# The first chunk of a fused recurrence and its inverse put ahead of the weight conversion in the opening

## The chip, the cores and the metric

The kernel runs on one core of a Trainium2 chip. The metric is the device time of one execution in microseconds (us). The core has a matrix engine (TensorE, PE), a vector engine (VectorE, DVE), a scalar engine (ScalarE, ACT), GpSimd (POOL) and SyncE (SP). They run their own instruction streams in order and wait for each other by semaphores. SP issues most transfers; ScalarE has a queue of its own for transfers too.

## The reference

Three parts follow each other. First a recurrence over 768 time steps for 4 batches and 8 heads with a 40 by 40 state, then two feed-forward parts on the 3072 tokens that it gives.

```
for t in range(S):                       # S = 768
    y[:, :, t] = r_t . state
    Sa = state . a_t
    state = state * w_t - outer(Sa, b_t) + outer(v_t, k_t)
x = y as 3072 x 320
x = ((x @ w_a) * (x @ w_b)) @ w_out      # w_a, w_b: 320 x 1536
out = gate * relu(x @ w1[e]) @ w2[e]     # e: the best of 8 experts of each token
```

## The kernel before, in words

The recurrence is computed in 12 chunks of 64 steps. What chunk c needs ahead of the state, the class `Attention` makes: it loads `w` and makes running products of it (`scans`, lines 493 to 498, DVE); scales `a` on POOL (`scale_a`) and spreads it by three transfers for each pair of batches into `ablk`; scales `bk` (`scale_bk`, line 527, DVE); multiplies them on PE (`scores`, line 537), copies the result out on ScalarE (line 545), masks it on POOL, and sends it to HBM (`nd`, line 552). From there it comes back in another layout as `m` (lines 600 and 605). `tinv` then inverts a triangular matrix by 31 pairs of a product and a difference on DVE (lines 614 and 620, so 62 steps that wait for each other); its result leaves through HBM (`td`, line 631) and comes back into `s` (line 635). `t21a` and `t21b` (a transpose on DVE at line 651, and products on PE) complete the inverse. `rows` makes transposed copies (`kb`), `relayout` moves running products into `gp` by six transfers, and `spans` checks on ScalarE that `w` lies in a range (line 474).

With these, `stage0` to `stage5` carry the state through chunk c for each of the four batches, mostly on PE, and give the tokens of the chunk (`xf`, line 816). The up-projection of a finished chunk, in groups of eight products (line 966), runs on PE while the next chunk goes through the recurrence; ScalarE copies one half out (line 969) and DVE multiplies it with the other (`uh`, line 978).

The weights `w_a` and `w_b` have to be split once into a high and a low part. `split64` does that in 30 pieces of 128 by 256, each in four steps on DVE (lines 364, 367, 376, 378), with a square, a check and casts on ScalarE (lines 365, 372, 374) and two instructions on POOL (380, 386). These are the 120 steps called `conv`. Raw data of a piece is loaded on ScalarE's queue into one of two or three buffers, so one or two pieces ahead.

`phase1` writes the order of the instructions by hand: first an opening, then a loop over the chunks, with 24 slots each. What stands in which slot is set by the tables STEADY and, for chunk 0, FIRST: `conv` says how many conversion steps, `tinv` how many steps of an inverse a slot holds; the conversion ends when its 120 steps are used up. In the opening before, 75 conversion steps are run, in part dealt between the steps of the inverses of chunks 0 and 1, which are both finished there; the other 45 follow in the loop, nearly all within chunk 0. Instructions of PE, DVE, ScalarE and POOL stay in this order; transfers on SP are put in order by a scheduler, and each of them uses one of eight completion lanes in turn and waits until the transfer before it on that lane has landed.

Of the kernel before, what the change touches and what calls it, by code (L numbers as in the profile page):

```python
# [21 lines left out]
C = 64  # L22
# [110 lines left out]
def phase1(tc, I, cst, drm, psA, psM, ident, hT, mk_ident, wo, xs, span, tiny, down):  # L133
# [66 lines left out]
    units, tinv = [], []  # L200
    for c in range(NCH + 1):
# [9 lines left out]
        for i in range(24):  # L211
# [76 lines left out]
            if 2 <= c < 10 and i == T["fill"]:  # L288
                if c == 2:
# [4 lines left out]
                    zt[:, None, :].to_broadcast([128, 2 * nz // XW, XW // 2]))  # L294
            n = T["tinv"][i]
# [14 lines left out]
    if not down:  # L310
# [40 lines left out]
def split64(nc, pool, raw, his, lo, dups=(), small=None):  # L351
# [1375 lines left out]
```

## Time and profile before

| | us |
|---|---|
| median of three runs | 1339.77 |
| lowest and highest | 1337.69, 1344.06 |
| the profiled execution | 1347.63 |
| its span, first to last instruction | 1345.9 |
| PE busy in the span | 1195.2 (89%) |
| DVE busy | 695.7 (52%) |
| ACT busy | 533.6 (40%) |
| POOL busy | 443.6 (33%) |

The profile is of one execution. Busy time is the time in which an engine ran an instruction; waiting and issuing of transfers are not counted. The median of the runs is the number to compare with; all shorter times are read from the profiled execution.

### The profile page before, as it was taken

The page shows a single profiled execution, that of the slowest core. Times are in us where ns is not written, and L with a number is a line of the kernel's source. Part 1 is how long each engine was busy: PE and PEld are TensorE (multiplying, and loading weights), DVE is VectorE, ACT ScalarE, POOL GpSimd, SP SyncE. Part 2 cuts the span into 40 slices and gives each one's busy share as a digit, 9 for nine tenths or more (in the row PEclk, how much of TensorE's full clock was granted, in tenths as well). Part 3 has the DMA queues.
Part 4 walks back from the last instruction along what each step waited for, and adds up shares of the span by engine and source line. Part 5 has one row for each costly group of instructions (what it writes and reads, how often), then busy time and mean ns, then how long its engine had stood idle before and what let it go on. Part 6 is the DMA issues. An engine that isn't in the chain of part 4 may idle for free. (4 is left out here: it accounts for less than half of the span.)

```text
span 1345.9 us, 27487 instructions
## 1 busy us (share of the span) xinstructions
PE 1195.2 (89%) x10474; PEld 1132.3 (84%) x10474; DVE 695.7 (52%) x1867; ACT 533.6 (40%) x1301; POOL 443.6 (33%) x488
## 2 busy tenths in 40 slices
PE   2306879999999999998999999999999989999995
PEld 2306769898898988998989899999999989999995
DVE  7487457563747475656664635312256685222321
ACT  3435544343433534353534232332333434444441
POOL 5443532231323233232321211112012255666650
PEclk9655559997989989999989897999799999999998
DMA  7363344446563856584754431217255635444410
GB/s 189 91 161 83 82 105 103 118 107 144 120 154 96 159 135 135 131 159 120 154 123 99 100 86 53 66 49 220 67 163 180 219 114 188 161 143 155 148 61 13
DMA packets 252909, 166.64 MB, mean 124 GB/s; under 512 B 158674, under 2 KB 236195, under 8 KB 252769
## 3 DMA queue, kind: packets, MB, share of 16 engines
q1 hardware_dynamic: 238545, 141.17, 41.4%
q0 software_dynamic: 9808, 15.76, 4.2%
q10 hardware_dynamic: 4416, 7.87, 2.1%
q8 instruction: 85, 1.39, 0.4%
q14 instruction: 55, 0.45, 0.1%
HBM read 111.76 MB, written 44.60 MB: 116 GB/s over the span
## 5 line engine op out<-in xcount | busy, mean ns | idle before, releaser
L978 DVE TENSOR_TENSOR uh<-pm,ua 128x256 f32<-128x256 f32 x144 | 60.6, 421 | 256.2 <-PE pm L966 237.0
L966 PE MATMUL pm<-xl,wh 128*128 128x256 f32 x576 | 137.6, 323 | 0.5 <-ACT ua L969 0.5
L614 DVE TENSOR_TENSOR tmp<-m,xt 128x126 f32<-128x126 f32 (+22 forms) x372 | 112.9, 306 | 30.3 <-DMA m<-nd 13.5
L620 DVE TENSOR_TENSOR xt<-xt,tmp 128x126 f32<-128x126 f32 (+22 forms) x372 | 121.5, 330 | 7.5
L966 PE MATMUL pm<-xh,wl 128*128 128x256 f32 x576 | 123.8, 299 | 0.0
L966 PE MATMUL pm<-xh,wh 128*128 128x256 f32 x576 | 122.6, 296 | 0.0
L784 POOL TENSOR_SCALAR_AFFINE_SELECT s<-s 64x512 f32<-64x512 f32 x96 | 71.9, 749 | 131.0 <-ACT s L782 126.6
L1395 DVE SCALAR_TENSOR_TENSOR hl<-u,hh 128x384 fp32r<-128x384 f32 (+5 forms) x72 | 41.5, 581 | 139.9 <-ACT hh L1394 139.9
L966 PEld LDWEIGHTS pm<-xl,wh 128*128 128x128 f32 x576 | 96.7, 208 | 3.4 <-ACT ua L969 0.7
L969 ACT COPY ua<-pm 128x256 f32<-128x256 f32 x144 | 53.7, 373 | 112.8 <-PE pm L966 108.7
L945 POOL TENSOR_TENSOR xl<-xf,xh 128x192 fp32r<-128x192 f32 x48 | 28.7, 600 | 210.9 <-ACT xh L944 189.3
L966 PEld LDWEIGHTS pm<-xh,wl 128*128 128x128 f32 x576 | 97.8, 208 | 0.0
L966 PEld LDWEIGHTS pm<-xh,wh 128*128 128x128 f32 x576 | 97.1, 207 | 0.0
L537 PE MATMUL s1p<-ablk,bk 120*128 120x192 f32 (+1 forms) x264 | 56.8, 361 | 44.3 <-DMA ablk<-at 28.1
L1103 PE MATMUL py<-wh,hl 128*128 128x328 f32 x288 | 90.9, 316 | 2.2 <-DVE hl L1093 2.2
L1103 PE MATMUL py<-wl,hh 128*128 128x328 f32 x288 | 92.1, 320 | 0.6 <-DVE wl L1074 0.6
L1103 PE MATMUL py<-wh,hh 128*128 128x328 f32 x288 | 90.6, 315 | 0.0
L537 PEld LDWEIGHTS s1p<-ablk,bk 120*128 120x128 f32 x264 | 50.0, 221 | 46.6 <-issue 45.9
L966 PE MATMUL pm<-xl,w 128*128 128x256 f32 x288 | 86.0, 299 | 0.0
L966 PE MATMUL pm<-xh,w 128*128 128x256 f32 x288 | 85.9, 298 | 0.0
L546 POOL TENSOR_SCALAR_AFFINE_SELECT s<-s 64x512 f32<-64x512 f32 x48 | 33.2, 697 | 136.1 <-ACT s L545 128.5
L1156 POOL DMA_INDIRECT xs<-xr,si x24 | 29.9, 1247 | 138.2 <-DVE acc L1151 87.7
(240 smaller groups left out, 3143.5 us busy)
## 6 DMA issues: line engine op xcount, KB each, us to landing
hT<-uh SPq DMA_DIRECT2D x72, 256.0 KB
hf<-hT SPq DMA_DIRECT2D x36, 512.0 KB
r<-in_moe_w SPq DMA_DIRECT2D x8, 1280.0 KB
r<-in_moe_w SPq DMA_DIRECT2D x8, 1024.0 KB
bk<-in_bk SPq DMA_DIRECT2D x11, 720.0 KB
xs<-zt SPq DMA_DIRECT2D x8, 805.0 KB
m<-nd SPq DMA_DIRECT2D x22, 256.0 KB
at<-in_a SPq DMA_DIRECT2D x24, 180.0 KB
```

The lines of the kernel that those rows point to most:

```text
L537: nc.tensor.matmul(ps[:2 * C, 3 * g * C:(3 * g + n) * C], st["bk5"](b, g), self.ablk[b // 2][:, b % 2, g, 0:n, 0:C], start=True, stop=True)
L546: nc.gpsimd.affine_select(out=s1[C:2 * C], in_=s1[C:2 * C], pattern=[[0, 8], [1, C]], base=0, channel_multiplier=-1, compare_op=ALU.is_gt, ...
L614: nc.vector.tensor_tensor(box[0], m[2 * s // R][:, s % (R // 2):s % (R // 2) + 1, s + 1:].to_broadcast([128, rows, n]), xt[:, :rows, s:s + ...
L620: nc.vector.tensor_tensor(xt[:, :rows, s + 1:], xt[:, :rows, s + 1:], box[0], op=ALU.subtract)
L784: nc.gpsimd.affine_select(out=s2t[q * C:q * C + C], in_=s2t[q * C:q * C + C], pattern=[[0, 8], [1, C]], base=0, channel_multiplier=-1, com ...
L945: nc.gpsimd.tensor_sub(xl[:, :, b, ts], xf, xh[:, :, b, ts].bitcast(F32))
L966: nc.tensor.matmul(p, l, r, start=(i == 0), stop=(i == len(seq) - 1))
L969: nc.scalar.copy(a, p)
L978: nc.vector.tensor_tensor(h[:, f % 2], p, a, op=ALU.mult)
L1103: self.nc.tensor.matmul(py, self.pair[i][l][:, k, s], self.W[r][:, first + k, cols], start=(first + k == 0 and n == 0), stop=(first + k == ...
L1156: self.nc.gpsimd.indirect_dma_start(self.xs[:], bass.IndirectOffsetOnAxis(ap=si[:, i:i + 1], axis=0), xr[:, j, :], None, bounds_check=NE * ...
L1395: nc.vector.scalar_tensor_tensor(out=hl, in0=p, scalar=0.0, in1=hh.bitcast(F32), op0=ALU.max, op1=ALU.subtract)
```

## The change

It touches the opening, the tables of chunk 0 and one tile of the conversion.

- Loads of the opening come in another order: `w` of chunk 0, its `a` and `bk`, then those of chunk 1.
- Three groups of transfers of chunk 0 are issued on ScalarE's queue instead of SP's: the spread of the second pair of `a`, the sends of `nd` and the loads of `m`.
- Scores of chunk 0 and the loads of its inverse stand ahead of the conversion, of which 15 steps are run in the opening. The 62 steps of inverse 0 then stand on DVE without anything between. Those of inverse 1 are dealt over slots 0 to 10 of chunk 0.
- Chunk 0's slots hold 51 conversion steps. The table of the later chunks deals the remaining 54 over slots 0 to 14 of chunk 1, which held none.
- The range check of chunk 0 moves from the opening to slot 23 of chunk 0, and loads `w` again there.
- Products of the second half of chunk 1's inverse (`t21a`, `t21b`) move to later slots of chunk 0.
- In the conversion, ScalarE's square gets a tile of its own (`ck`), where it used the one that DVE writes next.

```diff
+    A.load_w(0)
+    for pr in range(2):
+        A.load_a(0, pr)
+    A.load_bk(0)
...
+    A.scale_a(0, 1, queue=nc.scalar)
     run(A.scale_bk(0))
-    run(A.scans(1))
+    scans = A.scans(1)
+    for b in range(B):
+        A.scores(0, b, queue=nc.scalar)
+    tinv = A.tinv(0, queue=nc.scalar)
+    run(scans)
...
-    run(conv.take(n0))
-    for b in range(B):
-        A.scores(0, b)
-        if b % 2:
-            A.spread_a(1, b // 2)
-    run(conv.take(n1))
     for b in range(B):
         A.rows(0, b)
-    tinv = A.tinv(0)
-    run(conv.take(n2))
+    run(conv.take(FIRST["conv0"]))
...
-    mix(tinv[:n3], conv.take(FIRST["conv1"][0]) + [lambda b=b: A.rows(1, b) for b in range(B)])
     t1 = A.tinv(1, (uh, view(xt)))
-    A.relayout(0)
-    A.relayout(1)
-    lead = FIRST["lead"]
-    both = tinv[n3:n3 + lead]
-    tinv = tinv[n3 + lead:]
-    while tinv or t1:
-        both += tinv[:1] + t1[:1]
-        tinv, t1 = tinv[1:], t1[1:]
-    mix(both, [lambda b=b: A.stage0(0, b) for b in range(2)] + conv.take(FIRST["conv1"][1]))
-    run(A.spans(0, [t[:120, 0:L // 2].bitcast(F32) for t in sp]))
-    units, tinv = [], []
+    for b in range(2):
+        A.stage0(0, b)
+    run(tinv)
+    for b in range(B):
+        A.rows(1, b)
+    for c in range(2):
+        A.relayout(c)
+    tinv = t1
+    units = []
...
+            if c == 0 and i == FIRST["span0"]:
+                sp = [A.p2.tile([128, 2 * 256], F32, tag="raw", name=f"sp{h}")[:120, 0:L // 2] for h in range(2)]
+                run(A.spans(0, sp))
...
-    "conv0": [20, 5, 10, 16], "conv1": [10, 30], "lead": 5, "early": 12, "load": 0, "bk": 5, "sa": [3, 5], "score": [9, 12, 13, 15], "row": [12, 13, 23, 23],
-    "t21a": [8, 9, 14, 15], "t21b": [9, 12, 18, 16], "tinv": [0] * 24, "relayout": 17, "load_w": 18,
+    "conv0": 15, "span0": 23, "early": 12, "load": 0, "bk": 5, "sa": [3, 5], "score": [9, 12, 13, 15], "row": [12, 13, 23, 23],
+    "t21a": [14, 14, 17, 17], "t21b": [16, 16, 19, 19], "tinv": [5, 6, 6, 6, 6, 6, 6, 6, 6, 6, 3] + [0] * 13, "relayout": 17, "load_w": 18,
...
-    nc.scalar.activation(out=sq, in_=W.bitcast(F32), func=AF.Square)
+    ck = sq if small is None else pool.tile([128, n], F32, tag="ck", name="c_k", bufs=1)
+    nc.scalar.activation(out=ck, in_=W.bitcast(F32), func=AF.Square)
```

How this moves instructions shows at three places. In the rows that follow, names in front of `<-` are written, those behind it read, and numbers at their ends only tell tiles apart. The first place is ScalarE's stream in the opening. Before, the copies of chunk 0's scores (`s` from `s1p`) stand behind the casts of the fifth conversion piece, and behind them the next piece:

```order
L374 CAST w_0_249<-c_f 64x256 [waits DVE_49]
L374 CAST w_0_250<-c_f 64x256 x2
L384 CAST w_0_249<-c_f 64x256 [waits Pool_49]
L384 CAST w_0_250<-c_f 64x256 [waits Activation_49]
L545 COPY s_0_0_271<-s1p_0_267 128x512 [waits PE_49]
L545 COPY s_0_0_271<-s1p_1_274 128x512 [waits PE_49]
L545 COPY s_0_1_289<-s1p_2_285 128x512 [waits PE_49]
L545 COPY s_0_1_289<-s1p_3_292 128x512 [waits PE_49]
L872 DMA raw_1_0_303<-in_moe_w_b 128x512 [waits DMAHW1_49]
L365 ACTIVATE c_s<-raw_0_0_233 128x256 [waits DMAHW0_49]
L372 ACTIVATE c_s,tiny<-c_s,tiny 128x256 [waits Activation_49]
L374 CAST wh_0_192<-c_f 128x256 [waits DVE_49]
```

After, they stand with the sends of `nd` and the loads of `m` ahead of every piece:

```order
L546 COPY s_0_0_175<-s1p_0_171 128x512 [waits PE_49]
L546 COPY s_0_0_175<-s1p_1_178 128x512 [waits PE_49]
L553 DMA nd_118<-s_0_0_175 32x16x32 [waits DMAHW3_49,Activation_49]
L553 DMA nd_118<-s_0_0_175 32x16x32 [waits DMAHW6_49]
L546 COPY s_0_1_190<-s1p_2_186 128x512 [waits PE_49]
L546 COPY s_0_1_190<-s1p_3_193 128x512 [waits PE_49]
L553 DMA nd_118<-s_0_1_190 32x16x32 [waits DMAHW2_49,Activation_49]
L553 DMA nd_118<-s_0_1_190 32x16x32 [waits DMAHW5_49]
L606 DMA m_201<-nd_118 64x1x1024 [waits DMAHW7_49,DMAHW3_49,DMAHW2_49]
L606 DMA m_201<-nd_118 64x1x1024 [waits DMAHW6_49,DMAHW5_49]
L572 COPY kb_0_229<-kbp_0_225 128x360 [waits PE_49]
L572 COPY kb_1_235<-kbp_1_231 128x360 [waits PE_49]
```

The sends and loads have moved from SP's stream to ScalarE's, and the conversion is behind them.

The second place is SP's stream at the border of chunk 0 and chunk 1. Before, the load of `at`, which waits for PE's last `px` product, is followed by the sends of `gp`:

```order
L704 DMA uv_0_1531<-in_vt 120x3x64 [waits DMAHW5_49]
L457 DMA bk_1553<-in_bk 120x1536 [waits DMAHW6_49,DVE_49,PE_49]
L704 DMA uv_1_1564<-in_vt 120x3x64 [waits DMAHW7_49]
L507 DMA at_0_1596<-in_a 120x384 [waits DMAHW0_49,PE_49]
L584 DMA gp_1845<-w_1427 120x4x64 [waits DMAHW1_49,DVE_49]
L584 DMA gp_1845<-w_1427 8x4x64 [waits DMAHW2_49]
L584 DMA gp_1845<-w_1427 112x4x64 [waits DMAHW3_49]
```

After, the loads of the range check of chunk 0 (`sp`) stand behind it:

```order
L705 DMA uv_0_1363<-in_vt 120x3x64 [waits DMAHW1_49]
L457 DMA bk_1385<-in_bk 120x1536 [waits DMAHW2_49,PE_49]
L705 DMA uv_1_1406<-in_vt 120x3x64 [waits DMAHW4_49]
L504 DMA at_0_1454<-in_a 120x384 [waits DMAHW6_49,PE_49]
L585 DMA gp_1836<-w_1179 120x4x64 [waits DMAHW7_49,DVE_49]
L471 DMA sp_1335<-in_w 120x390 [waits DMAHW0_49,DMAHW3_49,DVE_49,Activation_49]
L585 DMA gp_1836<-w_1179 8x4x64 [waits DMAHW1_49]
L585 DMA gp_1836<-w_1179 112x4x64 [waits DMAHW2_49]
```

The two loads of the check (the second follows a few rows later) have come in between `gp` sends, behind the load that waits for PE.

The third place is DVE's stream in chunk 1, from its first product of the up-projection (`uh_0`, line 978 before, 979 after). Before, it is followed by steps of inverse 2 alone:

```order
L978 TENSOR_TENSOR uh_0_1637<-pm_0_1_1628,ua_0_1626 128x256
L614 TENSOR_TENSOR tmp_4_1660<-m_1503,xt_1504 128x81
L620 TENSOR_TENSOR xt_1504<-xt_1504,tmp_4_1660 128x3x27
L614 TENSOR_TENSOR tmp_5_1699<-m_1503,xt_1504 128x78
L620 TENSOR_TENSOR xt_1504<-xt_1504,tmp_5_1699 128x3x26
L614 TENSOR_TENSOR tmp_6_1702<-m_1503,xt_1504 128x100
L620 TENSOR_TENSOR xt_1504<-xt_1504,tmp_6_1702 128x4x25
L614 TENSOR_TENSOR tmp_7_1705<-m_1503,xt_1504 128x96
L765 TENSOR_TENSOR tp_0_1654<-pp_0_1650,bd 120x360
```

After, steps of inverse 2 and of the conversion (lines 367, 371, 380, 382) stand in turn:

```order
L979 TENSOR_TENSOR uh_0_1517<-pm_0_1_1508,ua_0_1506 128x256
L621 TENSOR_TENSOR xt_1315<-xt_1315,tmp_2_1533 128x2x29
L382 SCALAR_TENSOR_TENSOR c_s<-raw_0_0_1467,c_s 128x256
L615 TENSOR_TENSOR tmp_3_1551<-m_1314,xt_1315 128x56
L367 TENSOR_SCALAR c_f<-raw_0_1_1523 128x256
L621 TENSOR_TENSOR xt_1315<-xt_1315,tmp_3_1551 128x2x28
L371 SCALAR_TENSOR_TENSOR c_f<-raw_0_1_1523,c_f 128x256
L615 TENSOR_TENSOR tmp_4_1564<-m_1314,xt_1315 128x81
L380 TENSOR_SCALAR c_s<-c_f 128x256
L621 TENSOR_TENSOR xt_1315<-xt_1315,tmp_4_1564 128x3x27
L382 SCALAR_TENSOR_TENSOR c_s<-raw_0_1_1523,c_s 128x256
L615 TENSOR_TENSOR tmp_5_1607<-m_1314,xt_1315 128x78
```

Each step of the inverse has a step of the conversion beside it now, and the same `uh` products stand between them.

## Rows read from the trace of the kernel before

**Rows 1.** The page's slices of PE: 40 of 33.6 us, busy share in tenths.

```profile
PE   2306879999999999998999999999999989999995
```

**Rows 2.** Windows: busy time and count of each engine, granted clock, DMA.

```profile
100.00:110.00 10.00, 0.00 (x0) 0.00 (x0) 9.59 (x36) 2.86 (x8) 2.98 (x5) 0.50 0.50 103
200.00:210.00 10.00, 10.00 (x87) 9.74 (x87) 9.50 (x26) 3.36 (x8) 3.53 (x5) 1.00 0.24 64
```

**Rows 3.** Windows: chunk 0's loop, and chunk 1's first half.

```profile
111.30:187.60 76.30, 63.06 (x555) 57.59 (x555) 39.81 (x78) 41.85 (x123) 30.10 (x41) 0.54 0.39 92
187.60:223.20 35.60, 34.50 (x296) 32.21 (x295) 26.27 (x72) 13.49 (x36) 11.26 (x15) 0.85 0.36 93
```

**Rows 4.** Timeline, 20 to 80 us: start, duration, engine, work, [idle before and releaser].

```profile
21.83 3.75 PE L537 MATMUL s1p<-ablk,bk 120*128 120x192 f32 x12 [21.83 <-DMA ablk<-at]
...
37.78 2.05 ACT L545 COPY s<-s1p 128x512 f32<-128x512 f32 x4
...
44.04 1.31 SPq L605 DMA_DIRECT2D m<-nd  x2
...
60.39 0.19 DVE L614 TENSOR_TENSOR tmp<-m,xt 128x31 f32<-128x31 f32 x1 [11.53 <-DMA m<-nd]
...
61.45 2.24 SPq L600 DMA_DIRECT2D m<-nd  x4
63.74 10.93 SPq L584 DMA_DIRECT2D gp<-w  x5
...
74.80 0.38 DVE L614 TENSOR_TENSOR tmp<-m,xt 128x31 f32<-128x31 f32 x2 [1.94 <-DMA m<-nd]
```

**Rows 5.** Timeline: eight steps of inverse 0, and its way back.

```profile
70.12 0.26 DVE L620 TENSOR_TENSOR xt<-xt,tmp 128x100 f32<-128x100 f32 x1
...
72.57 0.29 DVE L620 TENSOR_TENSOR xt<-xt,tmp 128x126 f32<-128x126 f32 x1
...
103.44 2.63 SPq L631 DMA_DIRECT2D td<-xt  x4
...
111.28 0.75 DVE L651 STREAM_TRANSPOSE t<-s 32x256 f32<-32x256 f32 x2
```

**Rows 6.** Timeline of VectorE: one instruction of three conversion pieces.

```profile
23.26 0.42 DVE L367 SCALAR_TENSOR_TENSOR c_f<-raw,c_f 128x256 int32<-128x256 int32 x1
...
25.31 0.90 DVE L367 SCALAR_TENSOR_TENSOR c_f<-raw,c_f 128x256 int32<-128x256 int32 x1
...
27.83 0.90 DVE L367 SCALAR_TENSOR_TENSOR c_f<-raw,c_f 128x256 int32<-128x256 int32 x1
```

**Rows 7.** Timeline at the border of chunks 0 and 1.

```profile
168.72 0.36 SPq L448 DMA_DIRECT2D w<-in_w  x1
...
178.72 0.29 DVE L364 TENSOR_SCALAR c_f<-raw 128x256 int32<-128x256 int32 x1 [5.10 <-DMA raw<-in_moe_w_b]
...
179.70 0.61 ACT L474 ACTIVATE junk<-w,wlim 120x384 f32<-120x384 f32 x1 [5.16 <-DMA w<-in_w]
...
186.38 1.32 PE L715 MATMUL px<-sgT,at 120*64 120x120 f32 x6
...
195.16 0.79 PE L966 MATMUL pm<-xl,wh 128*128 128x256 f32 x2
```

**Rows 8.** Groups of VectorE by line, 0 to 257 us: the conversion.

```profile
L367 DVE SCALAR_TENSOR_TENSOR c_f<-raw,c_f 128x256 int32<-128x256 int32 x30 | 19.9, 664 | 0.6
L364 DVE TENSOR_SCALAR c_f<-raw 128x256 int32<-128x256 int32 x30 | 15.8, 527 | 6.5 <-DMA raw<-in_moe_w_b 5.1 <-POOL wl L386 1.4
L378 DVE SCALAR_TENSOR_TENSOR c_s<-raw,c_s 128x256 f32<-128x256 uint32 x30 | 13.8, 460 | 0.6
L376 DVE TENSOR_SCALAR c_s<-c_f 128x256 int32<-128x256 int32 x30 | 9.0, 300 | 30.3 <-ACT c_s L372 29.2
```

**Rows 9.** Timeline of VectorE: its sixth product of an up-projection in chunk 1.

```profile
223.22 0.43 DVE L978 TENSOR_TENSOR uh<-pm,ua 128x256 f32<-128x256 f32 x1 [1.52 <-PE pm L966]
```

**Rows 10.** Waits from 111 to 196 us: total, times, longest.

```profile
DVE c_s L376 <- ACT c_s L372: 22.0, 6, 6.4
```

More of the change, by code (lines that the diff above doesn't have):

```diff
@@ L149, in phase1 @@
     nz = NE * XCAP * XW // 128 // 8
-    sp = A.p2.tile([128, 2 * 256], I32, tag="raw", name="sp0"), A.p2.tile([128, 2 * 256], I32, tag="raw", name="sp1")
-    A.load(0)
-    A.load(1, M.room())
+    A.load_w(0)
+    for pr in range(2):
+        A.load_a(0, pr)
+    A.load_bk(0)
+    room = M.room()
+    A.load_w(1, room[0])
+    for pr in range(2):
+        A.load_a(1, pr)
+    A.load_bk(1, room[1])
     nc.scalar.activation(out=A.wlim, in_=A.wlim, func=AF.Copy)
@@ L159, in phase1 @@
     A.setup()
+    A.zero([A.vnt])
     run(A.spans(1))
     A.scale_a(0, 0)
-    A.scale_a(0, 1)
+    A.scale_a(0, 1, queue=nc.scalar)
     run(A.scale_bk(0))
-    run(A.scans(1))
+    scans = A.scans(1)
[3 more added lines that the diff above has]
+    run(scans)
     for pr in range(2):
-        A.scale_a(1, pr, spread=False)
+        A.scale_a(1, pr)
     run(A.scale_bk(1))
-    n0, n1, n2, n3 = FIRST["conv0"]
-    A.zero([A.vnt])
     A.begin(0)
@@ L371, in split64 @@
     else:
-        nc.scalar.activation(out=sq, in_=sq, func=AF.Relu, scale=-1.0, bias=small[0], accum_out=small[1])
+        nc.scalar.activation(out=ck, in_=ck, func=AF.Relu, scale=-1.0, bias=small[0], accum_out=small[1])
     for rows, h in list(his) + list(dups):
@@ L436, in src @@
         return self.I[name][c]
-    def load(self, c, room=None):
-        w, bk = room if room else (None, None)
-        self.load_w(c, w)
-        self.load_bk(c, bk)
     def load_w(self, c, room=None):
@@ L500, in scans, with load_a, scale_a @@
         ]
-    def scale_a(self, c, pr, spread=True):
+    def load_a(self, c, pr):
+        t = self.p2.tile([120, 6 * 64], F32, tag=f"at{pr}", name=f"at{c}_{pr}", bufs=2 + pr)[:, :6 * C]
+        self.nc.sync.dma_start(t, self.src("a", "a", c)[:, 6 * C * pr:6 * C * pr + 6 * C])
+        self.st[c]["raw_a", pr] = t
+    def scale_a(self, c, pr, queue=None):
         nc = self.nc
         st = self.st[c]
-        t = self.p2.tile([120, 6 * 64], F32, tag=f"at{pr}", name=f"at{c}_{pr}", bufs=2 + pr)[:, :6 * C]
-        sr = self.src("a", "a", c)[:, 6 * C * pr:6 * C * pr + 6 * C]
-        nc.sync.dma_start(t, sr)
+        if ("raw_a", pr) not in st:
+            self.load_a(c, pr)
+        t = st["raw_a", pr]
         tv = t.rearrange("p (s t) -> p s t", t=C)
@@ L511, in scale_a @@
         st["at"][pr] = t4
-        if spread:
-            self.spread_a(c, pr)
-    def spread_a(self, c, pr):
         for m in range(3):
-            self.nc.sync.dma_start(
+            (queue or nc.sync).dma_start(
                 self.ablk[pr][m * D:(m + 1) * D, :, :, m, 0:C], self.st[c]["at"][pr][m * D:(m + 1) * D])
@@ L529, in scale_bk, with scores @@
         return [lambda h=h, k=k: one(h, k) for h in range(2) for k in range(2)]
-    def scores(self, c, b):
+    def scores(self, c, b, queue=None):
         nc = self.nc
@@ L551, in send @@
                 q = slice(R * k, R * k + R)
-                nc.sync.dma_start(
+                (queue or nc.sync).dma_start(
                     st["nd"][k, 16 * pr:16 * pr + 16].rearrange("s j t -> j s t"),
@@ L584, in relayout, with tinv @@
             nc.sync.dma_start(gp[p0:p1, k, :, 0:C], v[q0:q0 + p1 - p0, :, g, :])
-    def tinv(self, c, room=None):
+    def tinv(self, c, room=None, queue=None):
         nc = self.nc
@@ L604, in tinv @@
             else:
-                nc.sync.dma_start(
+                (queue or nc.sync).dma_start(
                     t[64 * k:64 * k + 64],
```

2 lines of the change are left out of this document (removed), and 2 rows, old and new, of the table FIRST.

## The prediction, made before the changed kernel had run

> **What bounds the kernel now.** I read the page first: which engine is full, and where it is not. The slices of 33.6 us [rows 1] show TensorE (PE) at eight or nine tenths nearly everywhere from the fifth slice on, and at 2, 3, 0 and 6 tenths in the first four. So about the first 110 us are an opening without TensorE, and the rest is TensorE's. Windows of 10 us say the same [rows 2]: from 100 to 110 us PE is busy 0.00 and VectorE (DVE) 9.59, while from 200 to 210 us PE is busy 10.00 of 10. The granted clock is 0.50 in the first of these (1.2 GHz, the lower of its two levels) and 1.00 (2.4 GHz) in the second. The third view splits the part that the change touches [rows 3]: the loop of chunk 0 (111.30 to 187.60) has PE 63.1 and DVE 39.8 busy of 76.3 us, so DVE has 36 us free there; the first half of chunk 1 up to its sixth product of an up-projection (187.60 to 223.20) has PE 34.5 and DVE 26.3 busy of 35.6. So there are two places to cost: the time to the first PE work of the recurrence, and what is put into chunk 1, where PE is full and DVE has 9 us to spare.
>
> Next the single rows of the opening [rows 4]. TensorE's scores of chunk 0 are made at 21.83, but ScalarE copies them out only at 37.78, behind conversion pieces in its hand-written order. The loads of the inverse's matrix `m` are issued at 44.04, and DVE's first step of inverse 0 runs at 60.39, after 11.53 us of waiting for that load. Then inverse 0, inverse 1 and the conversion share DVE; the inverse of chunk 0 leaves at 103.44, comes back through HBM, and the transposes that let PE start run at 111.28 [rows 5].
>
> **The opening after the change.** Added here: nothing that computes. Moved: chunk 0's copies, sends and `m` loads go ahead of the conversion on ScalarE, and only 15 of 120 conversion steps stay ahead of the loop (75 before; 45 more were dealt into the loop's slots).
> - Scores stay at about 20 to 22. The copies (2.05 us for four) then follow at once. From copies to the end of the `m` issue took 37.78 to 45.35; I put copies at about 24 and the `m` loads at about 31, 13 us earlier.
> - Landing of `m`: no row shows it alone. From issue to first use it took 16.4 us (44.04 to 60.39), an upper bound since sends of chunk 1 ran beside it; inverse 1's loads took 13.3 (61.45 to 74.80) [rows 4]. I take 13, so it lands at 44; bounds 44 to 47.
> - The 15 conversion steps stand ahead of inverse 0 on DVE. Their raw loads are behind `m` on ScalarE's queue, the second of them on a completion lane that `m` used, so I let them start when `m` has landed. A piece of four steps took 2.5 us in the opening (from 25.31 to 27.83 for the same instruction of the next piece, [rows 6]): 15 steps are 9.5 us, to 53.5.
> - Inverse 0 alone: 62 steps. Eight steps without other work between took 2.45 us (70.12 to 72.57), 0.31 each [rows 5]; the short steps at both ends took 0.18, so I take 0.29: 18 us, to 71.5.
> - The way back and the transposes: 103.44 to 111.28, 7.8 us. PE starts at about 79.4 instead of 111.3: **32 us earlier**, between 26 and 37.
>
> The Trainium skill bears on one step of this. "DMA: Bandwidth & Descriptors", section "Queues, rings and completion order", says that each DMA engine takes one queue's descriptors in ring order; by it the raw loads cannot overtake `m` on ScalarE's queue. No row before shows a raw load behind an `m` load. If it did not hold, the first piece would be done before `m` lands, and PE would start 2.5 us earlier.
>
> **Chunk 0's loop.** From 111.30 to the last `px` product of chunk 1's first stage at 187.6 (PE, 186.38 plus 1.32, [rows 7]) it took 76.3 us. It gains 62 steps of inverse 1 on DVE (at 0.31, 19 us) and 7 more conversion steps; 39.8 plus 23 is 63 of 76, so DVE still has room. It loses the span check of chunk 0, eight ScalarE instructions (four checks and their accumulator reads) that ended just before DVE's scans of chunk 2; I credit 2 us. The later t21 products of chunk 1 (slots 14 and 17) still end ahead of their use. So the loop takes 74, and its end comes at about 153.5: **34 us earlier**.
>
> **What is given back.** Two terms, both at the border of chunks 0 and 1.
> - The span check sits in the last slot. Its two loads of w stand on SyncE behind the load of `at`, which waits for the same `px` product, and ScalarE does the checks, the next raw load, and then two `xs` copies, without which PE has no input, in that order. A load of w from issue (168.72) to its check (179.70) took 11.0 us [rows 7], but waited beside other traffic. Each is half of such a load: in proportion 5.5 us for the first and, sent behind a `gp` send, 9 for the second; then its checks (0.61 each [rows 7]) to 10.5, then the landing of the raw load, to about 13 to 14 us past the `px` product. Before, the first up-projection came 7.5 us after it (195.16); after, I expect 18. DVE, whose next row is the conversion piece that needs that raw load, idles up to about 13 us after the product. If each load took the whole 11.0, add 6; if they land in 3, take 4 off.
> - Chunk 1's first half then holds 52 conversion steps (13 pieces) ahead of, or dealt between, the products that feed PE. One piece over the opening and chunk 0 cost 19.9 + 15.8 + 13.8 + 9.0 = 58.5 us over 30 pieces [rows 8], 1.95 each, 0.49 a step: 25.4 us. What DVE did there before is 26.3 us [rows 3]. Together 51.7: DVE becomes the bound from 13 us past the product, and its use of the sixth up-projection (223.22 [rows 9], 35.6 past the border before) comes at 13 + 51.7 = 64.7, 29 us later relative to the border. Its bounds are in the rivals B and C.
> - The rest of chunk 1, from the seventh up-projection on, is unchanged and TensorE's.
>
> The private tile for ScalarE's squares takes away waits of DVE for ScalarE (22.0 us in six waits from 111 to 196 us, [rows 10]). They lay in stretches in which DVE had nothing urgent; in chunk 1 the tile saves DVE from waiting on ScalarE inside a piece, which is why I use busy time alone. I cost it at nothing; without that cover a wait of 3 us a piece would come on top. Chunks from 2 on do not change.
>
> **Sum.** -34 + 29 = -5 us against the profiled execution's 1347.63: 1342.6. That execution lies 7.9 us above the median of the three runs (1339.77), so the median goes to about **1335**.
>
> **Rivals.**
> - *A, the forecast*: 1335, own range 1326 to 1343, chance 0.40.
> - *B, the conversion hides better.* Uncontended, one of its instructions took 0.42 us, beside GpSimd 0.90 [rows 6]. Its mean is 0.66 [rows 8]; if the whole piece shrinks in that ratio, 13 pieces are 16 us instead of 25.4, and if the span check's loads land fast the idle time is 4 us less: give-back 16 and total -18, about 1321. For it: in chunk 1 GpSimd is busy only 11.3 of 35.6 us [rows 3]. Against: each piece brings its own GpSimd work. Chance 0.27. "SBUF — State Buffer", section "Who interferes with whom", of the Trainium skill says that a VectorE instruction with two inputs in SBUF contends with a GpSimd instruction that reads it; the 0.42 against 0.90 agrees, and by that rule the contention comes along with the pieces, so it speaks for A's price.
> - *C, the other side: slower.* Only one piece of raw data is loaded ahead. A raw load once held DVE for 5.10 us [rows 7]. If every piece in chunk 1 waits so, the loads set the pace, 5 us a piece with the other work inside: 13 pieces are 65 us, the sixth comes 78 past the border, 43 later, and the total is +9: 1349. The point from which it decides is 34 + 35.6 - 13 = 57 us for the 13 pieces, 4.4 each. A starved TensorE might also stay at the lower clock of the opening [rows 2] for longer. Against: loads of the opening kept up with 2.5 us a piece. Chance 0.23.
> - *D, the change doesn't do what it says in the opening.* The inverse's way back is on SyncE, behind twelve `gp` sends (five took 10.93, [rows 4]), chunk 1's spreads, sends and `m` loads. About 26 + 6 + 8 + 2 us of issues from 23 on end near 65; every landing waited for on a lane adds to that. If the way back leaves at 81 instead of 71.5, PE starts at 89 and the total is +4: 1344. Chance 0.10.
>
> **Numbers.** About 0.5%, 6.7 us, is what a measurement of this kernel can tell from no change: faster lies below 1333.1, slower above 1346.5. A stands near that edge: 0.17 faster, 0.23 the same. B is faster, 0.27. C is 0.17 slower and 0.06 the same; D 0.04 slower and 0.06 the same. That makes 0.44, 0.35 and 0.21. The range takes in B's middle and C's middle with a little of each: 1313 to 1351.
>
> **What would show it.** In the profile after: PE's first `ta` at about 79 (74 to 85), `m` issued near 31, DVE's inverse steps running alone from 53 to 72; the first up-projection some 18 us behind the last `px` of chunk 0's loop, with ScalarE waiting for w; chunk 1's first six products spread over 45 to 50 us and DVE nearly full there; chunk 2 on as before. Wrong it would be if PE's first work comes later than 90 (D), if DVE waits for raw in chunk 1 again and again (C), or if PE stays full through chunk 1 (B).

## The result, and the profile after

The changed kernel takes 1349.62 us in the median of 20 runs, the kernel before 1340.05 us in the median of 20 beside them: a ratio of 1.0061, 95% interval 1.0042 to 1.008. By this ratio it is slower by some 8 us (the two medians differ by 9.6), where the forecast was 5 us faster. Its profiled execution took 1350.41 us with a span of 1348.7.

The page's slices of PE (33.7 us each, busy share in tenths), to be held against [rows 1]:

```profile
PE   2347657999999989999999999999999989999995
```

PE has 2, 3, 4, 7 tenths in its first four slices where it had 2, 3, 0, 6: it starts earlier. But the fifth, sixth and seventh are 6, 5 and 7 where they were 8, 7 and 9: what came in front is missing behind. Four moments show where. The table gives them in us, from the timelines of this kernel, of the one before (see [rows 5, 7, 9]) and of all kernels of the experiments below. "ta" is the start of PE's first product of the chain, "px" the end of the last px product of chunk 0's loop, "up" the start of the first up-projection, "sixth" the start of DVE's sixth product of chunk 1:

| kernel | ta | px | up | sixth | ratio to before, 95% |
|---|---|---|---|---|---|
| before | 111.9 | 187.7 | 195.2 | 223.2 | 1 |
| changed | 84.6 | 164.9 | 183.3 | 232.3 | 1.0061 [1.0042, 1.008] |
| e1_check_later | 83.6 | 164.2 | 174.2 | 223.3 | 1.0002 [0.9973, 1.0031] |
| e2_raw_first | 83.5 | - | - | - | 1.0076 [1.0039, 1.0112] |
| e3_sp_queue | 74.7 | 162.2 | 180.4 | 229.4 | 1.0116 [1.0077, 1.0154] |
| e4_tile_alone | 109.7 | 178.5 | 185.8 | 214.5 | 0.9965 [0.9933, 0.9997] |
| e5_conv_ahead | 105.2 | 172.1 | 182.1 | 228.3 | 1.0107 [1.0055, 1.0158] |
| e6_inverse_ahead | 95.3 | 169.7 | 187.7 | 236.6 | 1.0134 [1.0075, 1.0193] |
| e7_tile_undone | 84.0 | 166.9 | 186.8 | 237.3 | 1.0127 [1.0074, 1.018] |
| e8_tile_check_deal | 109.5 | 176.0 | 182.2 | 216.6 | 0.9957 [0.9926, 0.9988] |
| e9_opening_filled | 75.7 | 159.6 | 168.6 | 210.3 | 0.9933 [0.9898, 0.9969] |
| e10_all_in_chunk0 | 76.3 | 173.8 | 186.4 | 214.7 | 0.991 [0.9871, 0.9948] |
| e11_tile_again | 109.5 | 180.2 | 187.5 | 216.0 | 0.9976 [0.9944, 1.0007] |

The profiled execution of e2_raw_first was one of the slow runs, so only its opening is used.

Against before the changed kernel is 27 us ahead at ta, 23 at px, 12 at up, and 9 us behind at the sixth product. That 9 us lies near the 8 us of the ratio, but one moment of one execution is no proof of a median. At the fourteenth product the same two executions lie 17 us apart (283.0 and 266.3): these eight products take 50.8 us with PE at a granted clock of 0.80, where before they took 43.1 at 1.00. At their ends the two lie 2.8 us apart. The better support is the table as a whole: of the kernels with a sixth product in it, all but e3 and e5 are as much longer or shorter in total as at the sixth product, within 5 us; in these two the total is 9 us longer than it tells.

The windows between these four moments (busy time and count of PE, PEld, DVE, ACT, POOL, then granted clock and DMA) answer to [rows 3]:

```profile
84.60:164.90 80.30, 60.55 (x556) 55.68 (x557) 58.61 (x141) 40.33 (x117) 31.46 (x43) 0.59 0.38 93
164.90:183.30 18.40, 6.53 (x53) 5.78 (x52) 8.43 (x15) 10.70 (x32) 6.20 (x9) 0.50 0.39 101
183.30:232.30 49.00, 38.61 (x292) 35.62 (x292) 45.25 (x112) 26.86 (x80) 27.49 (x34) 0.82 0.40 110
```

Chunk 0's loop takes 80.3 us with PE busy 60.6 of them; between px and up PE is busy 6.5 of 18.4; from up to the sixth product it takes 49 us with DVE busy 45.3 of them, where before the whole stretch from px to the sixth product was 35.6 us with PE busy 34.5 of them.

The opening, from the timelines of ScalarE, DVE, SyncE and PE, answers to [rows 4, 5]:

```profile
22.95 0.59 ACT L546 COPY s<-s1p 128x512 f32<-128x512 f32 x1 [8.63 <-PE s1p L538]
...
30.16 1.64 ACTq L606 DMA_DIRECT2D m<-nd  x2
...
31.94 0.89 ACTq L873 DMA_DIRECT2D raw<-in_moe_w_a  x1
...
47.14 0.29 DVE L367 TENSOR_SCALAR c_f<-raw 128x256 int32<-128x256 int32 x1 [25.50 <-DMA raw<-in_moe_w_a]
...
54.93 0.29 DVE L367 TENSOR_SCALAR c_f<-raw 128x256 int32<-128x256 int32 x1 [4.79 <-DMA raw<-in_moe_w_b]
...
58.41 0.18 DVE L615 TENSOR_TENSOR tmp<-m,xt 128x31 f32<-128x31 f32 x1
...
78.31 2.63 SPq L632 DMA_DIRECT2D td<-xt  x4
...
84.04 0.76 DVE L652 STREAM_TRANSPOSE t<-s 32x256 f32<-32x256 f32 x2 [5.75 <-DMA s<-td]
...
84.62 1.88 PE L655 MATMUL ta<-t,s 32*32 32x32 f32 x32 [20.90 <-DVE t L652]
```

Copies at 22.95 and the `m` loads at 30.16, as forecast. But the first raw load, issued at 31.94 behind them, holds DVE until 47.14, and a later one costs 4.79 us more; DVE stands still for 25.50 us in a row. ScalarE, which also issues these loads, sends the second at 40.44 and the third only at 48.07. Inverse 0 starts at 58.41 and the transposes run at 84.04, not 79.4.

The border, in order of time, answers to [rows 7, 9]:

```profile
162.80 0.85 PE L728 MATMUL sgp<-ident,sgT 120*120 120x120 f32 x3 [8.38 <-DVE xf L817]
163.58 1.33 PE L716 MATMUL px<-sgT,at 120*64 120x120 f32 x6
...
168.13 0.49 SPq L471 DMA_DIRECT2D sp<-in_w  x1
...
170.89 0.62 ACT L474 ACTIVATE junk<-sp,wlim 120x384 f32<-120x384 f32 x1 [2.76 <-DMA sp<-in_w]
...
172.36 0.34 SPq L471 DMA_DIRECT2D sp<-in_w  x1
...
175.18 0.61 ACT L474 ACTIVATE junk<-sp,wlim 120x384 f32<-120x384 f32 x1 [2.84 <-DMA sp<-in_w]
...
176.66 0.33 ACTq L873 DMA_DIRECT2D raw<-in_moe_w_b  x1
...
178.76 1.93 PE L738 MATMUL pu<-xs,s 64*64 64x40 f32 x16 [10.09 <-ACT xs L723]
...
179.52 0.63 DVE L367 TENSOR_SCALAR c_f<-raw 128x256 int32<-128x256 int32 x1 [8.94 <-DMA raw<-in_moe_w_b]
...
183.27 0.79 PE L967 MATMUL pm<-xl,wh 128*128 128x256 f32 x2
...
232.25 0.41 DVE L979 TENSOR_TENSOR uh<-pm,ua 128x256 f32<-128x256 f32 x1
```

ScalarE gets the two halves of w at 170.89 and 175.18, and only then issues the raw load (176.66) that DVE has waited for 8.94 us, and makes the copy that PE has waited for 10.09 us. The first up-projection is at 183.27, 18.4 us behind the px product.

Last the conversion on DVE, by line, 0 to 260 us ("x30 | busy, mean ns | idle before us <-releasers"), to be held against [rows 8]:

```profile
L371 DVE SCALAR_TENSOR_TENSOR c_f<-raw,c_f 128x256 int32<-128x256 int32 x30 | 20.4, 681 | 0.7
L367 DVE TENSOR_SCALAR c_f<-raw 128x256 int32<-128x256 int32 x30 | 15.2, 506 | 57.0 <-DMA raw<-in_moe_w_a 34.7 <-DMA raw<-in_moe_w_b 22.3
...
L382 DVE SCALAR_TENSOR_TENSOR c_s<-raw,c_s 128x256 f32<-128x256 uint32 x30 | 14.7, 489 | 0.5
L380 DVE TENSOR_SCALAR c_s<-c_f 128x256 int32<-128x256 int32 x30 | 11.4, 381 | 0.6
```

Work is much the same: 61.7 us for the 30 pieces, 58.5 before. What changed is the idle time: before, 30.3 us ahead of line 376, for ScalarE (29.2 of it), and 6.5 ahead of line 364, of which 5.1 for raw data; now 0.6 ahead of line 380 and 57.0 ahead of line 367, for raw data alone. One wait took the place of another.

### The profile page after: what moved, and what is told of

Same layout as the page of the kernel before. It is cut to its first block, busy times and chain, and to the rows that moved or that the text cites. A ratio compares the mean times of both kernels' runs of the same rounds, so it can differ in the third digit from the quotient of the medians.

```text
span 1348.7 us, 27467 instructions
## 1 busy us (share of the span) xinstructions
PE 1192.5 (88%) x10474; PEld 1129.3 (84%) x10474; DVE 706.1 (52%) x1867; ACT 532.1 (39%) x1301; POOL 436.8 (32%) x488
## 4 chain that ended last, share of the span: by engine, by line
PE 63%; DVE 14%; DMA 13%; issue 4%; ACT 2%; POOL 2%; SPq 1%; POOLq 0%; ACTq 0%; DVEq 0%
PE pm L967 18%; PE py L1104 8%; PE dn L1413 6%; PE u L1393 6%; PE py L800 3%; DVE tmp L615 3%; PE s1p L538 3%; PE px L719 3%; DVE xt L621 3%; PE pu L738 2%; DMA hT<-uh 2%; PE py L796 2%; PE px L716 2%; PE pp L760 2%; PE p L778 2%
## 5 line engine op out<-in xcount | busy, mean ns | idle before, releaser
L979 DVE TENSOR_TENSOR uh<-pm,ua 128x256 f32<-128x256 f32 x144 | 60.6, 421 | 245.3 <-PE pm L967 227.0
L615 DVE TENSOR_TENSOR tmp<-m,xt 128x126 f32<-128x126 f32 (+22 forms) x372 | 116.4, 313 | 18.0 <-DMA xt<-in_one 7.2
L547 POOL TENSOR_SCALAR_AFFINE_SELECT s<-s 64x512 f32<-64x512 f32 x48 | 33.7, 704 | 129.4 <-ACT s L546 122.0
L1413 PE MATMUL dn<-l,hh 128*128 128x320 f32 (+3 forms) x240 | 74.9, 312 | 0.0
```

The costliest lines, as they stand in the source:

```text
L615: nc.vector.tensor_tensor(box[0], m[2 * s // R][:, s % (R // 2):s % (R // 2) + 1, s + 1:].to_broadcast([128, rows, n]), xt[:, :rows, s:s + ...
L979: nc.vector.tensor_tensor(h[:, f % 2], p, a, op=ALU.mult)
L1413: nc.tensor.matmul(p, l[:, q], r[:, f], start=(f == 0 and i == 0), stop=(f == len(hs) - 1 and i == 2))
```

## The experiments

**The range check moved out of the border.** e1_check_later:

```diff
-            if c == 0 and i == FIRST["span0"]:
+            if c == 2 and i == 1:
```

> The changed kernel with the range check of chunk 0 (its two loads of w and four checks) moved from slot 23 of chunk 0 to slot 1 of chunk 2; nothing is left out. Theory (the border and chunk 1's conversion give back what the opening gains, and the border's part is this check on ScalarE): the first up-projection follows the last px product of chunk 0's loop by about 8 us instead of 18.4, DVE's long wait for raw (8.9 us) is gone, and the total falls by 8 to 11 us against the changed kernel, to about 0.998 of the kernel before. Rival (VectorE's conversion is what chunk 1 waits for, and the check lies in its shadow): the first up-projection comes earlier, but the sixth product of chunk 1 stays within 3 us of 232, and the total stays at about 1.006 of before.

Measured 1.0002 [0.9973, 1.0031]. PE and DVE at the border:

```profile
162.82 1.33 PE L716 MATMUL px<-sgT,at 120*64 120x120 f32 x6
...
169.45 1.93 PE L738 MATMUL pu<-xs,s 64*64 64x40 f32 x16 [1.53 <-ACT xs L723]
...
174.16 0.79 PE L967 MATMUL pm<-xl,wh 128*128 128x256 f32 x2
...
223.32 0.42 DVE L979 TENSOR_TENSOR uh<-pm,ua 128x256 f32<-128x256 f32 x1
```

The up-projection comes 10.0 us behind the px product, and the sixth product at 223.3, 8.9 us earlier than in the changed kernel. DVE's wait of 8.9 us for raw is gone; the longest there is 0.9. The theory holds: the check costs 9 us at the border, all of it is still there at the sixth product, and the total falls by 0.6%.

**Raw loads ahead of the m loads.** e2_raw_first:

```diff
     scans = A.scans(1)
+    for j in range(3):
+        M.load_raw(j)
     for b in range(B):
         A.scores(0, b, queue=nc.scalar)
```

> The changed kernel with the loads of the first three raw pieces issued on ScalarE's queue ahead of chunk 0's score copies, so ahead of the nd sends and m loads; nothing else differs. Theory (in the opening the 15 conversion steps wait for raw loads that stand behind m on the same queue, 25.5 us of idle DVE): the conversion runs while m is under way, inverse 0 starts at about 45 instead of 58.4, PE's first ta comes at about 72 instead of 84.6, and the total falls by 6 to 12 us against the changed kernel. Rival (m itself, and its transfers' contention, sets the start; raw loads ahead push m back by what they take): PE's first ta stays within 4 us of 84, and the total is unchanged.

Measured 1.0076 [1.0039, 1.0112]. DVE, and one row of ScalarE's queue:

```profile
21.57 0.29 DVE L369 TENSOR_SCALAR c_f<-raw 128x256 int32<-128x256 int32 x1
...
44.55 0.35 ACTq L876 DMA_DIRECT2D raw<-in_moe_w_b  x1
...
52.02 0.29 DVE L369 TENSOR_SCALAR c_f<-raw 128x256 int32<-128x256 int32 x1 [9.83 <-DMA raw<-in_moe_w_b]
...
82.95 0.76 DVE L654 STREAM_TRANSPOSE t<-s 32x256 f32<-32x256 f32 x2 [9.18 <-DMA s<-td]
```

Two pieces are converted from 21.57 on. But scores come 4.6 us later (25.5; they wait for `ablk`, whose transfers now share the time with the raw loads), and `m` is issued at 34.9. DVE starts the third piece only at 40.65, after 16.1 us behind GpSimd's `wl`, which itself waits for ScalarE's cast behind the sends and `m` loads. The fourth piece's load, issued at 44.55, lands 7.5 us later. Inverse 0 starts 5.4 us earlier (53.0), its way back takes longer (9.2 us for 5.8), and PE starts 1.1 us earlier. The rival's forecast is right: ta stays within 4 us. Its reason fits only in part, since the last wait ahead of inverse 0 is for raw data and not for `m`.

**The transfers back on SyncE's queue.** e3_sp_queue (three such lines):

```diff
-        A.scores(0, b, queue=nc.scalar)
+        A.scores(0, b)
```

> The changed kernel with the three groups of transfers of chunk 0 (spread of the second pair, nd sends, m loads) back on SyncE's queue; the order of the engines' work stays. Theory (the gain of the opening is from the order on ScalarE, not from the queue; the queue costs, because raw loads stand behind m on it): m is issued within 3 us of 30, raw loads land before m, the conversion is done when m lands, and PE's first ta is at 74 to 82 instead of 84.6; total 2 to 8 us below the changed kernel. Rival (ScalarE's queue is what brings m forward, since SyncE has the gp and spread transfers ahead of it): m is issued 8 us or more later, PE's first ta comes after 90, total 5 us or more above the changed kernel.

Measured 1.0116 [1.0077, 1.0154]. ScalarE's queue, SyncE's queue and DVE:

```profile
27.66 0.39 ACTq L873 DMA_DIRECT2D raw<-in_moe_w_a  x1
...
29.76 1.50 SPq L606 DMA_DIRECT2D m<-nd  x2
...
30.59 0.29 DVE L367 TENSOR_SCALAR c_f<-raw 128x256 int32<-128x256 int32 x1 [8.95 <-DMA raw<-in_moe_w_a]
...
31.39 0.34 ACTq L873 DMA_DIRECT2D raw<-in_moe_w_b  x1
...
39.43 0.30 DVE L367 TENSOR_SCALAR c_f<-raw 128x256 int32<-128x256 int32 x1 [2.35 <-DMA raw<-in_moe_w_b]
...
47.04 0.19 DVE L615 TENSOR_TENSOR tmp<-m,xt 128x31 f32<-128x31 f32 x1 [6.52 <-DMA m<-nd]
```

`m` is issued at 29.8, as early as on ScalarE's queue, so the queue brought nothing forward. The first raw load now lands 2.9 us after its issue (27.66 to 30.59), where behind `m` it took 15.2 (31.94 to 47.14). But it also goes out 2.1 us before `m`, as ScalarE no longer issues the sends and `m`. The load that goes out 1.6 us after `m`, on the other queue, took 8.0 (31.39 to 39.43); in the changed kernel the first load went out 1.8 us after `m`, on the same queue. As far as three single loads can tell, order in time and the shared queue both count: 2.9, 8.0 and 15.2 us. The conversion is done before `m` is there, and PE starts at 74.7. In the opening the theory is right. Of the 10 us that it gains, 2.7 are left at px and 2.9 at the sixth product: the loop, 87.5 us, swallows the rest. The total is not 2 to 8 us below that of the changed kernel, as the theory had it, but above; it doesn't follow from these moments. The loss lies in later chunks, in which both kernels do the same, and stays open. What is on record is the clock: the median of its six executions is granted 0.897, that of the changed kernel's 0.902.

**The private tile alone.** e4_tile_alone, on the kernel before; e11_tile_again is the same kernel once more beside later ones:

```diff
-    nc.scalar.activation(out=sq, in_=W.bitcast(F32), func=AF.Square)
+    ck = sq if small is None else pool.tile([128, n], F32, tag="ck", name="c_k", bufs=1)
+    nc.scalar.activation(out=ck, in_=W.bitcast(F32), func=AF.Square)
```

> The kernel before with only the private tile for ScalarE's squares in the conversion. Theory (the waits that it removes lay where DVE had nothing urgent): between 0.997 and 1.002 of before; DVE's waits for ScalarE inside a piece (22 us from 111 to 196 us) are gone, and the first up-projection stays within 3 us of 195. Rival (these waits held back the end of chunk 0's loop, since xf and the scans stand behind them on DVE): first up-projection 4 us or more earlier, total 0.996 or less.

> The kernel before with the private tile alone, once more, beside the two others on one chip. Theory: the first up-projection at 184 to 188 as before, total 0.994 to 0.999 of before. Rival (the first measurement was chance): total 0.999 to 1.003 and the first up-projection at 190 or later.

Measured 0.9965 [0.9933, 0.9997] and 0.9976 [0.9944, 1.0007]. Chunk 0's loop:

```profile
109.70:178.50 68.80, 54.36 (x556) 49.52 (x556) 40.34 (x76) 41.06 (x122) 29.30 (x41) 0.65 0.43 102
```

It takes 68.8 us instead of 75.9 (111.85 to 187.7), in e11 70.7; ta comes 2 us earlier, and the sixth product 7 to 9 us earlier. In its moments the rival of e4 is right, and the theory of e11: the waits of [rows 10] are gone, and the loop is shorter. The tile is worth some 0.3%, though one of the two intervals reaches across 1. That the waits held the chain is not shown. PE stood still in the loop for 14.4 us (e4) and 11.0 (e11), for 12.7 before, and its wait for `xf` was 7.3 and 7.6 us, 6.0 before. What fell was PE's busy time for the same products: 54.4 us at a granted clock of 0.65 and 59.7 at 0.57, where before it was 63.2 at 0.55. Whether the tile raised the clock, by the way it spread PE's work, stays open.

**No conversion in chunk 0's loop.** e5_conv_ahead ("conv" of FIRST is all zeros):

```diff
+    run(conv.take(41))
     tinv = t1
```

> The changed kernel with no conversion step in chunk 0's slots: 41 steps (10 pieces and a step) run between inverse 0 and the loop, the other 64 in chunk 1. Of interest is the length of chunk 0's loop, from PE's first ta to the end of the last px product: 80.3 us in the changed kernel (84.6 to 164.9), 69 in the kernel before with the tile alone. Theory (the conversion in the slots stretches it: each piece waits for its raw load, and xf, masks and copies stand behind pieces): 70 us or less. Rival (the steps of inverse 1 dealt between do it): 76 or more. The time as a whole: 1.005 to 1.02 of before, since PE starts some 20 us later and chunk 1 holds 10 steps more.

Measured 1.0107 [1.0055, 1.0158], with this loop:

```profile
105.20:172.10 66.90, 56.83 (x556) 52.36 (x557) 35.48 (x95) 25.29 (x69) 13.76 (x22) 0.60 0.30 66
```

66.9 us instead of 80.3, as the theory forecast. But this loop also starts 20.6 us later, and in e3, with the slots unchanged, a loop that started 9.9 us earlier was 7.2 us longer. So this run doesn't separate the conversion from the start. The comparison at an equal start is that of e9 and e10 below.

**Inverse 1 ahead of the loop.** e6_inverse_ahead ("tinv" of FIRST is all zeros):

```diff
-    tinv = t1
+    run(t1)
+    tinv = []
```

> The changed kernel with all 62 steps of inverse 1 run on DVE behind inverse 0, ahead of the loop, instead of dealt over slots 0 to 10. Theory (the conversion stretches chunk 0's loop): PE's first ta comes 14 us later, at about 98, and the loop shortens by 5 us at most, so the last px product ends at 172 to 176 (164.9 in the changed kernel); total 1.010 or more of before. Rival (inverse 1 stretches it): the loop shortens by 10 us or more, the last px product ends at 168 or less, total 1.008 or less.

Measured 1.0134 [1.0075, 1.0193], with this loop:

```profile
95.30:169.70 74.40, 57.26 (x556) 52.55 (x557) 40.57 (x79) 40.62 (x117) 31.41 (x43) 0.59 0.39 95
```

74.4 us, so 5.9 less, with px at 169.7. Neither forecast fits whole. Here too the loop starts later, by 10.7 us, and going by e3 the start alone could make this difference; what inverse 1 costs in the slots is not shown. ta came at 95.3 and not 98, with DVE at work on inverse 1 while inverse 0 was on its way through HBM.

**The tile undone in the changed kernel.** e7_tile_undone:

```diff
-    ck = sq if small is None else pool.tile([128, n], F32, tag="ck", name="c_k", bufs=1)
+    ck = sq
```

> The changed kernel with ScalarE's squares back in the tile that DVE writes next. Theory (the tile is worth 9 us in the kernel before, by 0.9965 and an up-projection that starts 9.4 us earlier; the changed kernel holds this gain, so the rest of the change costs 15 us or more): 8 to 20 us slower than the changed kernel, 1.012 to 1.02 of before, DVE waits for ScalarE's L372 again inside pieces. Rival (the tile matters only where pieces follow each other without other work between): within 4 us of the changed kernel, 1.003 to 1.009.

Measured 1.0127 [1.0074, 1.018]. DVE's wait for ScalarE, 84 to 240 us (total, times, longest):

```profile
DVE c_s L380 <- ACT c_s L376: 29.4, 12, 8.9
```

The waits are back, 29.4 us in twelve. The sixth product comes 5 us later and the total is 9 us above that of the changed kernel, at the lower edge of what the theory expects and with intervals that overlap. In chunk 0's loop, one wait again took the place of the other: 14.0 us for ScalarE, but 4.7 for raw data instead of 14.9, and the loop is 2.6 us longer. Without the tile the change would have cost some 1.3%.

**Part of the change on the kernel before.** e8_tile_check_deal has the tile, the check in chunk 2, and 17 steps of the conversion left to chunk 1, where the kernel before leaves one (28 in chunk 0; the expectation counts 29 and 16):

```diff
-        0, 3, 3, 2, 3, 2, 2, 2, 2, 1, 2, 2,
-        2, 2, 2, 4, 1, 1, 3, 0, 3, 0, 1, 1],
+        0, 1, 2, 1, 2, 1, 1, 2, 1, 1, 1, 1,
+        1, 2, 1, 3, 1, 1, 1, 0, 2, 0, 1, 1],
```

> The kernel before with the private tile, the range check of chunk 0 in slot 1 of chunk 2, and 16 of the 45 conversion steps of the loop left to chunk 1 (29 in chunk 0 and 16 in chunk 1's first slots). Nothing is left out. Theory (few steps fit beside PE's work in chunk 1, where DVE has 9 us free, and the check's 5 us on ScalarE at the opening's end go): the last px product 5 to 9 us earlier than with the tile alone (178.5), the sixth up-projection product 3 to 9 us earlier than 214.5, total 0.990 to 0.996 of before. Rival (each step moved to chunk 1 comes back there): the sixth product stays at 213 to 217, total 0.995 to 0.998.

Measured 0.9957 [0.9926, 0.9988]. px is 2.5 us earlier than with the tile alone, the sixth product 2.1 later. By these moments the rival is right, and what leaves chunk 0 comes back in chunk 1; the total lies in both ranges. The loop, with 16 steps fewer and the same start, is 66.5 us, 2 to 4 shorter than in e4 and e11: a step costs 0.14 to 0.26 us there, about half of its busy time or less.

**The opening filled.** e9_opening_filled takes the changed kernel with the edits of e1 and e3, and puts conversion where DVE stood still in the opening; e10_all_in_chunk0 has 77 steps in chunk 0's slots besides:

```diff
-    "conv0": 15, "span0": 23,
+    "conv0": 28, "span0": 23,
...
     run(tinv)
     for b in range(B):
         A.rows(1, b)
+    run(conv.take(12))
```

> The changed kernel with all three lessons at once: the three groups of transfers back on SyncE's queue, the range check of chunk 0 in slot 1 of chunk 2, and the conversion put where DVE idles in the opening (28 steps while m is under way, 12 while inverse 0 goes through HBM), so that chunk 1 holds 29 steps instead of 54. Nothing is left out. Theory (what counts is DVE's idle time ahead of chunk 1's sixth up-projection product, and each of the three costs adds up): sixth product at 208 to 216 (232.2 in the changed kernel, 214.5 in the kernel before with the tile alone), total 0.990 to 0.997 of before. Rival (chunk 0's loop swallows what the opening gains, as it did with SyncE's queue alone): sixth product at 218 or later, total 0.998 to 1.004.

> As e9_opening_filled, but with 77 conversion steps in chunk 0's slots instead of 51, so that only 3 are left to chunk 1. Theory (DVE is the limit on both sides of the border, so a step costs about the same in chunk 0 as in chunk 1): the last px product 8 to 15 us later than in e9_opening_filled, the sixth up-projection product within 4 us of it. Rival (chunk 1 is the dearer place, because PE is full there): the sixth product 5 us or more earlier than in e9_opening_filled.

Measured 0.9933 [0.9898, 0.9969] and 0.991 [0.9871, 0.9948]: both beat the kernel before and the changed one. The theory is right for e9 (sixth product at 210.3). In e10 px is 14.2 us later and the sixth product 4.4 us later, just outside the 4 that the theory allows and against the rival: a step costs a little more in chunk 0 than in chunk 1. The two totals can't be told apart, and their intervals also overlap with those of the tile alone (e4, e11).

The two loops start within 0.6 us of each other and differ by 26 conversion steps:

```profile
75.70:159.60 83.90, 60.88 (x556) 55.86 (x557) 57.01 (x143) 42.98 (x124) 31.54 (x45) 0.58 0.50 118
76.30:173.80 97.50, 63.60 (x556) 58.41 (x556) 70.17 (x167) 50.54 (x148) 41.52 (x58) 0.54 0.48 120
```

The loop grows by 13.6 us, 0.52 a step, and DVE's busy time in it by 13.2, while DVE stands still for 27 us in both. So with inverse 1 dealt in beside them, conversion steps cost chunk 0 their full busy time, although DVE has time to spare.

What all of these have in common shows in DVE's time up to the sixth product. Before:

```profile
0.00:223.20 223.20, 118.50 (x954) 109.39 (x954) 145.70 (x365) 99.06 (x275) 95.46 (x127) 0.67 0.48 118
```

Changed:

```profile
0.00:232.30 232.30, 124.66 (x1001) 115.23 (x1002) 153.26 (x362) 95.92 (x271) 88.60 (x124) 0.68 0.46 113
```

e9_opening_filled:

```profile
0.00:210.30 210.30, 117.70 (x955) 108.48 (x955) 155.21 (x366) 96.47 (x267) 91.24 (x127) 0.68 0.50 124
```

DVE is busy 145.7, 153.3 and 155.2 us, so it stands still for 77.5, 79.0 and 55.1 us. The sixth product comes at the sum. The change moved DVE's idle time about and added 8 us of busy time, nearly all of it in steps that took longer: those of the inverses 60.0 us for 55.1, the conversion's line 380 11.2 for 9.0. Why they took longer is not shown; GpSimd was busy less than before (88.6 us for 95.5). e9 took idle time away.

## Why the prediction was wrong

Working by its own steps, in us to the sixth product:

- **The opening**: -32 forecast, -27 measured (transposes at 84.0, not 79.4). `m` was issued within 1 us of the forecast. Inverse 0 with its way back took 25.6 us for 25.8, which was luck: the inverse took 19.9 for 18, the way back 5.7 for 7.8. The step that failed is the raw loads' landing: at 47.1 and not at 44, with a second wait of 4.8 behind it. The conversion itself was quicker, 6.5 us for 9.5, and hid 3 of these 8. The direction of the failure had been seen: 47 was the outer bound for the landing of `m`. e3 shows that the raw loads' place behind `m` costs PE's start 9.9 us: a raw load took 2.9 us ahead of `m`, 8.0 behind it on another queue and 15.2 behind it on the same. By the Trainium skill, "DMA: Bandwidth & Descriptors", section "Queues, rings and completion order", each DMA engine takes the descriptors of a queue in ring order; the 15.2 against 8.0 us agree.
- **Chunk 0's loop**: the step "the loop takes 74" failed; it took 80.9 from the transposes on. Against before, PE was busy 2.6 us less (at a granted clock of 0.59 for 0.55) and stood still 7.1 us more. The step was argued from DVE's busy time, 63 of 76 us, and that was the mistake: DVE had the time, and e10 against e9 shows that added steps cost their full busy time all the same. One term was misread besides: the 2 us credited for the range check of chunk 0. The checks that end just before DVE's scans of chunk 2 read `w` [rows 7]; they are chunk 2's and stay. Those of chunk 0 read `sp` and ran from 110.6 to 113.6. Waits in the loop of the changed kernel (total, times, longest):

```profile
DVE c_f L367 <- DMA raw<-in_moe_w_b: 8.6, 2, 5.9
PE sgp L728 <- DVE xf L817: 8.4, 1, 8.4
...
DVE c_f L367 <- DMA raw<-in_moe_w_a: 6.3, 2, 5.0
PE py L800 <- POOL s L785: 5.9, 2, 3.8
```

  DVE waits 14.9 us for raw data, PE 8.4 for `xf` on DVE (6.0 before) and 5.9 for a mask on GpSimd (0.5 before). That the hand-written order puts a raw wait in front of what PE needs fits these rows, but is argued and not shown: e5 and e6 have shorter loops that also start later, and no run gives the loop its raw data earlier with all else the same.
- **The tile at nothing**: wrong too, and in the other direction. By e4 and e11 the sixth product comes 7 to 9 us earlier with it and the loop is 5 to 7 us shorter, the larger part of it PE's busy time at a higher granted clock. So the loop may hide two errors of opposite sign: against the kernel before with the tile (68.8 and 70.7 us) the changed loop is 10 to 12 us longer, of which PE's standing still is 5 to 9.
- **The border**: up at 18 us behind px forecast, 18.4 measured, with the mechanism forecast; e1 shows that it is the check. Inside it two sizes were off and made up for each other: a load of the check took 2.8 us from issue, not 5.5, but the two were issued 3.2 and 7.5 us behind px.
- **Chunk 1**: 46.7 us from up to the sixth product forecast, 49.0 measured, DVE busy for 45.3 of them. DVE was nearly full there, as forecast, and the price of 0.49 us a step was near the 0.52 measured (25.8 us for 50 steps). The step "the rest of chunk 1 is unchanged" didn't hold in the profiled execution, by the 50.8 us for 43.1 at the lower clock told above.

So the give-back of 29 us was 32, while of the 34 us that were to be gained 23 came. -34 + 29 became -23 + 32 = +9. The sign turned on the loop (7 us) and on the raw loads in the opening (5); either alone would have left a change too small to tell from none. Rival C gave the time, 1349, but by luck. It named raw loads that set the pace, and put them in the wrong place: from up to the sixth product DVE waited for them 2.1 us, in the opening and in chunk 0's loop 30 and 15. Its 65 us for the 13 pieces of chunk 1 were 52.7, near the forecast's 51.7. D didn't happen: SyncE sent the way back at 78.31, right behind inverse 0.

## What to carry to other kernels

Before work is dealt into another engine's slots by its free time, look at what each of its instructions waits for and what stands behind it: here conversion steps cost their full busy time in a loop in which DVE stood still for 27 us. To bring one chain forward is worth little by itself: PE's start 10 us earlier (e3) moved the sixth product by 2.9 us, while e9, which also moves the check and fills DVE's idle time in the opening, moved it by 22. And a queue on which a slow transfer goes out first is no place for loads that the next engine needs.

## What the runs showed of the hardware that I had not expected

A chunk in which PE is nearly full and the instructions are the same takes very different times. In one execution of e11_tile_again, two chunks of 683 instructions of PE each:

```profile
250.60:329.30 78.70, 72.71 (x683) 68.11 (x682) 42.57 (x113) 29.07 (x80) 20.36 (x26) 0.85 0.51 110
398.20:462.10 63.90, 62.54 (x683) 58.53 (x683) 41.85 (x114) 29.05 (x80) 20.70 (x26) 1.00 0.73 155
```

78.7 us at granted clock 0.85 with PE busy 72.7, and 63.9 us at 1.00. Which chunk gets the low stretch differs from kernel to kernel, and single executions of a kernel spread over 7 to 23 us. The longer ones are those with the lower clock: the changed kernel's 20 go from 1338.55 us at a granted clock of 0.907 to 1355.43 at 0.899. Comparisons of a few us therefore rest on moments ahead of the first full chunk, which came within 2 us where a kernel was profiled twice (e4 and e11), and on medians of many runs.

That a load of 256 KB behind `m` takes 15.2 us on the same queue, where it takes 8.0 behind it on another and 2.9 ahead of it, was larger than I had thought. "DMA: Bandwidth & Descriptors" of the Trainium skill, section "Issuing engines are not separate DMA queues", says that issuing from several engines saves issue time only. No run here measures bandwidth by queue; but which loads stand behind which was worth 10 us at ta.
